# A long convolution in front of a maxout network: second and third transform stage of batches 1 to 3 as 64x64 products

## The chip, the cores and the metric

The kernel runs on one core of a Trainium2 chip. The metric is the device time of one launch in microseconds (us); less is better. The engines of the core are TensorE (PE in the profile, with its weight loads as PEld), VectorE (DVE), ScalarE (ACT), GpSimd (POOL) and SyncE (SP, which here only issues transfers).

## The reference

A causal convolution over the whole sequence of 12544 positions, for each of 128 channels and 4 batches, gated by x, and then a maxout network on each of the 50176 tokens. All arrays are float32.

```python
batch, seq, d_model, filter_order = 4, 12544, 128, 64
h_filt = (np.maximum(pos_emb @ w1, 0) @ w2) * np.exp(-0.01 * pos)[:, None]
u = x * v
Uf, Hf = rfft(u, n=2 * S, axis=1), rfft(h_filt, n=2 * S, axis=0)
y = irfft(Uf * Hf[None], n=2 * S, axis=1)[:, :S]
a = (x * y).reshape(50176, 128)
out = np.maximum(np.maximum(a @ moe_w1, a @ moe_w2), a @ moe_w3) @ moe_w_out   # 768 hidden units
```

## The kernel before

**The transform.** The sequence is seen as 98 blocks of 128 positions. The first stage (`u_first`, `first_halves`) is a product over the 98 blocks into 90 frequencies; its result lies in the tile `spec`, 128 partitions by 90 frequencies by 2 by 128 channels. The second stage runs over the 128 partitions (real and imaginary part of 64 values) for two frequencies at a time, a pair; there are NK = 45 pairs in a batch. For a pair `g_second` makes eight products of 128x64 by 128 columns (`halves_mm`: two products of 64 output rows each, one beside the other), `g_butterfly` adds and subtracts the halves, `g_swap` (two copies on ACT), `g_re` and `g_im` multiply by the filter's spectrum, `g_unfold` adds and subtracts again, and `g_third` makes eight products back. Its result goes to DRAM (`zd`, one tile for each batch). The last stage, `t_last`, takes four positions by 98 blocks of one batch from there (`t_load`: the `zt` part from `zd` and `xT`, the part of x), makes sixteen short products and multiplies by x. That tile of 392 tokens, `gt`, is what the network works on.

**The network.** A tile has six slots, one for each 128 of the 768 hidden units. In a slot `up` makes two products of 392 columns (`pa`, `pb`); ACT takes the relu of the one and DVE the maximum with the other, and `down`, one slot later, adds the third product to the output's PSUM tile `ops` (with `lin` once in a tile). There are NT = 32 tiles in a batch.

**The order.** Instructions stand in the order of the program (`manual_schedule`); each engine does its own in that order. Batch 0 is transformed by itself in a prologue, to about 320 us, together with the filter's spectrum, which goes to `hd` in DRAM. In that stage `s_filter` makes sixteen products of 64x64 by 128 columns for each pair. After that the tiles of batches 0, 1 and 2 run, and beside the tiles of batch b the transform of batch b + 1: `conv_steps` hands out a list of steps for each of the batch's 192 slots, and the main loop runs them after the slot's `up` and `down`. Its places come from one line and a few offsets: the first stage of the 32 column groups u (26 in batch 1, six are done in the prologue) one after the other, then the pairs.

```python
per_pair = 170 / (NK + 0.6 * (NU - done))
s0 = int((NU - done) * 0.6 * per_pair) + 10
s = s0 + int(g * per_pair)
at(s - 5, 0, w_load, g, 0); at(s - 3, 0, h_load, g); at(s, 1, g_second, g)
at(s + 1, 0, w_load, g, 1); at(s + 1, 0, g_butterfly, g); at(s + 2, 0, g_swap, g)
at(s + 3, 0, g_re, g); at(s + 4, 0, g_im, g, True); at(s + 6, 0, g_unfold, g)
at(s + 7, 1, g_third, b, g)
```

Loads are issued by SP (`u_load`, `w_load`, `h_load`, `t_load`, the transposes of `u_dma`), the stores of `zd` and of the output by ACT. The first-stage, second-stage, third-stage and `t_last` results share a pool of four PSUM buffers (`cps`, 512 columns each); `pa` and `pb` share three; `ops` has one. The tiles of batch 3 run last, in pairs of tiles, with a form of the network that has fewer products and sums on POOL.

In batches 1 to 3, `g_third` forms sum and difference of its two halves on its way out, so that `t_last` can use them as they come. For batch 0 `t_sums` does that after the load, on POOL.

Of the kernel before, what the change touches and what calls it, by code (L numbers as in the profile page):

```python
# [15 lines left out]
P = 128  # L16
# [24 lines left out]
def tables(NB):  # L41
# [4 lines left out]
    f1 = np.concatenate([a.real, a.imag], 1)  # L46
    f1h = np.zeros((64 + HH, 2 * N1))
    f1h[:HH], f1h[64:] = f1[:HH], f1[HH:NH]
    f4 = np.stack([a.T.real, a.T.imag], 1) / S
    f4p = f4[::2].transpose(1, 0, 2).reshape(N1, NB // 2, 2).transpose(0, 2, 1)  # L50
    j, t = np.arange(64), np.arange(64)
# [13 lines left out]
    both = both.reshape(N1 // 2, P, 2, 512)  # L65
    f32 = np.float32
    return f1.astype(f32), f1h.astype(f32), f4p.astype(f32), np.ascontiguousarray(both, f32)
# [3 lines left out]
def kernel(  # L71
# [32 lines left out]
    zd = [dram.tile([N1, 2, 64, 256], FP32, name=f"zd{b}") for b in range(B)]  # L104

    f1_t, f1h_t, f4p_t, w_t = tables(NB)
# [3 lines left out]
    wt_d = nc.inline_tensor(w_t, name="wt_const").ap()  # L110
    order = 127 - (2 * np.arange(64)[None, :] + np.arange(2)[:, None]).ravel()
# [6 lines left out]
    f1 = const.tile([NB, 2 * N1], FP32, name="f1")  # L118
# [153 lines left out]
    nc.gpsimd.dma_start(f1[:], f1_d)  # L272
# [40 lines left out]
    us, uts, ws, hts, eos, xts, xss, abs_, pss = ({} for _ in range(9))  # L313

    def pools(b, u):
        if b == 0:
            return inp0 if u % 2 else inp
        return inp if u < EARLY or u % 5 < 3 else inq
# [20 lines left out]
    def u_turn(u):  # L339
        if u % 2 == 0:  # L340
            uts[u] = uts[u + 1] = utp.tile([NB, 8, 2, 64], FP32, tag="uT", name="uT")
        ps = state["turn"].tile([P, 512], FP32, tag="cv", name="pst")
        turn(u, ps)
        nc.scalar.copy(uts[u][:, 4 * (u % 2):4 * (u % 2) + 4],
                       ps[0:NB, :].rearrange("n (s t r) -> n s r t", s=4, r=2))
# [16 lines left out]
    def u_join(u):  # L362
        if u % 2 == 0:
            uts[u] = uts[u + 1] = utp.tile([NB, 8, 2, 64], FP32, tag="uT", name="uT")
        t = us.pop(u)
        for h in range(2):
            copies[h](
                uts[u][:, 4 * (u % 2):4 * (u % 2) + 4].rearrange(
                    "n s r t -> n (s r t)").bitcast(U16).rearrange(
                    "n (s r t h) -> n h s r t", h=2, r=2, t=64)[:, h],  # L370
                t[0:NB, 4 * h:4 * h + 4].rearrange("n s (t r) -> n s r t", r=2))

    def u_first(u, h, copy=None):
        t = uts[u] if h == 0 else uts.pop(u)
        ps = cps.tile([P, 512], FP32, tag="cv", name="ps1")
        at = 4 * u + 2 * h
        first_halves(ps, [t[:, at % 8 + j] for j in range(2)], f1[:], spec[:, :, :, at:at + 2],
                     copy or copies[h])

    def w_load(g, a):  # L380

        w = state["pair"][0].tile([P, 2, 2, P], FP32, tag=f"w{a}", name="wt")
        nc.sync.dma_start(w[:].rearrange("p k r m -> p (k r m)"), wt_d[g, :, a, :])
        ws[g, a] = w

    def h_load(g):
        ht = state["pair"][1].tile([P, 2, 2, 2, D], FP32, tag="h", name="ht")
        for half in range(2):
            nc.sync.dma_start(
                ht[64 * half:64 * half + 64].rearrange("p c k q d -> p c (k q d)"),  # L390
                hd[g].rearrange("(c j) f -> j c f", c=2))
        hts[g] = ht

# [37 lines left out]
    def g_third(b, g):  # L431
# [7 lines left out]
        if b == 0:  # L439
            nc.scalar.copy(zs[:].rearrange("p k f -> p (k f)"), ps[:])  # L440
        else:
            z1 = state["cv"][0].tile([P, 256], FP32, tag="z1", name="z1", bufs=1)
            nc.scalar.copy(z1[:], ps[:, 256:512])  # L443
            for a, op in enumerate((ALU.add, ALU.subtract)):
                nc.vector.tensor_tensor(out=zs[:, a], in0=ps[:, 0:256], in1=z1[:], op=op)  # L445
        nc.scalar.dma_start(
            zd[b][2 * g:2 * g + 2].rearrange("k c t f -> (c t) k f"), zs[:])

    def conv_steps(b, done):
# [9 lines left out]
        per_pair = 170 / (NK + 0.6 * (NU - done))  # L459
        for u in range(done, NU):  # L460
            s = (u - done) * 0.6 * per_pair + 9
            at(max(0, int(s) - 10), 0, u_load, b, u)
# [4 lines left out]
            for h in range(2):  # L467
                at(int(s + 1 + 0.3 * per_pair * h), 1, u_first, u, h)
        s0 = int((NU - done) * 0.6 * per_pair) + 10
        for g in range(NK):  # L470
            s = s0 + int(g * per_pair)
            at(s - 5, 0, w_load, g, 0)
            at(s - 3, 0, h_load, g)
            at(s, 1, g_second, g)
            at(s + 1, 0, w_load, g, 1)
            at(s + 1, 0, g_butterfly, g)
            at(s + 2, 0, g_swap, g)
            at(s + 3, 0, g_re, g)
            at(s + 4, 0, g_im, g, True)
            at(s + 6, 0, g_unfold, g)  # L480
            at(s + 7, 1, g_third, b, g)
# [10 lines left out]
    def t_load(b, i):  # L492
        zt = hp.tile([N1, 2, 512], FP32, tag="zt", name="zt", bufs=2)
        for c in range(2):
            nc.sync.dma_start(
                zt[NK * c:NK * c + NK],
                zd[b].rearrange("(g a) c t f -> g a c t f", a=2)[
                    :, :, c, 2 * i:2 * i + 2, :].rearrange("g a t f -> g a (t f)"))
# [6 lines left out]
    def t_sums(i, eng=nc.gpsimd):  # L505
        if i[0]:
            return
# [485 lines left out]
```

## Time and profile before

| | |
|---|---|
| timed runs | 2401.75 us median of 3 (2400.04 to 2402.64) |
| profiled execution, span from first to last instruction | 2397.1 us (no other time is given for it) |
| mean granted TensorE clock | 0.997 |
| transfers | 408.43 MB, mean 170 GB/s |
| matmul groups: `pa`, `pb`, `ops` with `hid` (392 columns) | 643.5, 642.7, 481.2 us busy |
| second and third stage, all four batches (L130, `ps`) | 193.9 and 191.5 us busy, 2880 records each |
| first stage (L139, `ps`), 4096 records | 188.9 us busy |
| `sps` of `s_filter` (L788), 1440 records | 49.7 us busy |

The busy time of a group is the union of its records. Matmuls overlap, so a group's mean duration isn't what an additional one costs; the distance between the starts of groups is. A float32 matmul and its weight load show as two records each. In the views of transfers, "issue" is the time that SP or ACT spends on a transfer's instruction, and "landing" the time until its data is there. The busy shares leave these issues out.

### The profile page before, as it was taken

To read this page: it belongs to the slowest core of one execution; us is meant where nothing else is said; L and a number is where in the kernel's file an instruction comes from. 1 tells how busy PE (TensorE), PEld (TensorE's weight loads), DVE (VectorE), ACT (ScalarE), POOL (GpSimd) and SP (SyncE) were. 2 spreads that over 40 slices of the span, in tenths; PEclk is the share of its full clock that TensorE was granted. 3 is DMA by queue.
4 is the path that set the end of the run, shared out by engine and by line. 5 is a ranking of instruction groups with operands and counts; after the bars stand their busy time and mean duration, and the time that the engine had idled before them with its cause. 6 is when DMAs were issued, how large, how long until landed. Compare 5 with 4: busy or idle time off the path is not lost.

```text
span 2397.1 us, 67636 instructions
## 1 busy us (share of the span) xinstructions
PE 2366.6 (99%) x27853; PEld 1514.6 (63%) x27853; DVE 1318.5 (55%) x2806; ACT 1018.9 (43%) x1978; POOL 704.1 (29%) x775
## 2 busy tenths in 40 slices
PE   9999999999999999999999999999999999999998
PEld 7889856656555556666655546666665645666665
DVE  5588844466666645446666644546666643333333
ACT  2688834444444434444444424444444432222222
POOL 2055432222323211101111111101111105666666
PEclk9999999999999999999999999999999999999999
DMA  7778978868787659968778859978778842222221
GB/s 173 178 230 269 278 162 173 171 185 215 205 215 208 181 128 189 182 172 211 215 206 215 216 129 182 180 165 216 214 210 220 203 134 55 68 56 55 66 64 21
DMA packets 532221, 408.43 MB, mean 170 GB/s; under 512 B 375859, under 2 KB 421996, under 8 KB 531913
## 3 DMA queue, kind: packets, MB, share of 16 engines
q1 hardware_dynamic: 422240, 315.25, 55.0%
q10 hardware_dynamic: 100233, 67.88, 9.8%
q0 software_dynamic: 9440, 20.98, 3.6%
q8 instruction: 219, 3.59, 0.6%
q14 instruction: 89, 0.73, 0.1%
HBM read 295.69 MB, written 84.67 MB: 159 GB/s over the span
## 4 chain that ended last, share of the span: by engine, by line
PE 91%; ACT 3%; DMA 2%; issue 1%; DVE 1%; POOL 1%; ACTq 0%; SPq 0%; POOLq 0%; DVEq 0%
PE pb L130 21%; PE pa L130 21%; PE ops L130 18%; PE ps L130 11%; PE ps L139 7%; PE ops L601 5%; PE yps L130 5%; ACT ht L793 1%; PE pm L299 1%; DMA hd<-ht 1%; PE pst L337 1%; PE pw L130 1%; ACT zs L440 1%; PE gps L770 0%; ACT xs L409 0%
## 5 line engine op out<-in xcount | busy, mean ns | idle before, releaser
L541 DVE TENSOR_TENSOR hid<-hid,pb 128x392 f32<-128x392 f32 x768 | 431.4, 562 | 725.9 <-PE pb L130 492.2
L538 ACT ACTIVATE hid<-pa 128x392 f32<-128x392 f32 x768 | 381.8, 498 | 789.6 <-PE pa L130 616.3
L130 PE MATMUL pb<-gt,w_sb 128*64 128x392 f32 x3072 | 642.7, 494 | 4.4 <-ACT hid L538 4.2
L130 PE MATMUL pa<-gt,w_sb 128*64 128x392 f32 x3072 | 643.5, 494 | 0.8 <-DVE gt L528 0.8
L130 PE MATMUL ops<-hid,wo_sb 128*64 128x392 f32 x2304 | 481.2, 492 | 0.0
L420 POOL TENSOR_TENSOR xt<-xt,xs 128x512 f32<-128x512 f32 x135 | 172.5, 1278 | 889.8 <-DVE xs L419 662.8
L130 PEld LDWEIGHTS pb<-gt,w_sb 128*64 128x64 f32 x3072 | 227.7, 137 | 286.1 <-issue 251.0
L130 PEld LDWEIGHTS ops<-hid,wo_sb 128*64 128x64 f32 x2304 | 173.4, 137 | 205.8 <-issue 162.0
L130 PEld LDWEIGHTS pa<-gt,w_sb 128*64 128x64 f32 x3072 | 202.9, 137 | 61.5 <-issue 34.3
L139 PEld LDWEIGHTS ps<-f,uT 98*64 98x64 f32 x4096 | 178.5, 137 | 47.5 <-issue 44.0
L130 PEld LDWEIGHTS ps<-ab,wt 128*64 128x64 f32 x2880 | 166.2, 137 | 48.0 <-issue 30.3
L130 PEld LDWEIGHTS ps<-spec,wt 128*64 128x64 f32 x2880 | 171.9, 137 | 38.7 <-issue 34.8
L130 PE MATMUL ps<-spec,wt 128*64 128x128 f32 x2880 | 193.9, 273 | 1.9 <-issue 1.4
L130 PE MATMUL ps<-ab,wt 128*64 128x128 f32 x2880 | 191.5, 274 | 0.0
L352 POOL COPY planes<-ut 128x784 uint16<-128x784 uint16 x90 | 76.3, 848 | 388.8 <-DVE ut L332 246.1
L139 PE MATMUL ps<-f,uT 98*64 98x90 f32 x4096 | 188.9, 241 | 0.4 <-ACT zs L440 0.3
L445 DVE TENSOR_TENSOR zs<-ps,z 128x256 f32<-128x256 f32 x270 | 101.9, 419 | 96.7 <-ACT z L443 94.5
L130 PEld LDWEIGHTS yps<-f4p,zt 90*64 90x64 f32 x3584 | 134.0, 138 | 25.9 <-issue 22.0
L409 ACT ACTIVATE xs<-xt 64x512 f32<-64x512 f32 x180 | 113.1, 629 | 71.7 <-DVE xt L156 58.9
L427 DVE TENSOR_TENSOR ab<-xt 128x256 f32<-128x256 f32 x360 | 135.9, 419 | 4.5
L130 PE MATMUL yps<-f4p,zt 90*64 90x49 f32 x3584 | 137.3, 221 | 0.4 <-DVE zt L511 0.4
L528 DVE TENSOR_TENSOR gt<-yps,xT 128x392 f32<-128x392 f32 x128 | 72.5, 566 | 111.3 <-PE yps L130 62.3
(114 smaller groups left out, 2544.5 us busy)
## 6 DMA issues: line engine op xcount, KB each, us to landing
wt<-wt_const SPq DMA_DIRECT2D x360, 256.0 KB, 4.8
ht<-hd SPq DMA_DIRECT2D x270, 256.0 KB, 4.9
zd<-zs ACTq DMA_DIRECT2D x180, 256.0 KB, 4.7
zt<-zd SPq DMA_DIRECT2D x256, 180.0 KB, 4.2
ut<-in_xr_dram SPq DMA_DIRECT2D x128, 196.0 KB, 3.7
ut<-in_vr_dram SPq DMA_DIRECT2D x128, 196.0 KB, 4.1
xT<-in_x_dram SPq DMA_DIRECT2D x512, 49.0 KB, 2.8
out_dram<-ot ACTq DMA_DIRECT2D x96, 196.0 KB, 4.4
```

Source lines behind the costliest of these rows:

```text
L130: nc.tensor.matmul(out[64 * h:64 * h + 64], lhsT[:, 64 * h:64 * h + 64], rhs, start=start, stop=stop, skip_group_check=True)
L139: nc.tensor.matmul(ps[64 * c:64 * c + 64, 256 * i + r * N1:256 * i + (r + 1) * N1], a[:, r, :], table[:, c * N1:(c + 1) * N1], start=(i % ...
L299: nc.tensor.matmul(ps[64 * h:64 * h + HH, 512 * r + q * FO:512 * r + (q + 1) * FO], posv[64 * h:64 * h + 64, P - 1 - 2 * (8 * i + q) - r, ...
L352: nc.gpsimd.tensor_copy(pl_[:, :, :, 0:NB], a[:].bitcast(U16).rearrange("p s (n h) -> p h s n", h=2))
L409: nc.scalar.mul(xs[0:64], xt[64:128], -1.0)
L420: (nc.gpsimd if apart else nc.vector).tensor_tensor(out=xt[:], in0=xt[:], in1=xs[:], op=ALU.add)
L427: nc.vector.tensor_tensor(out=ab[:, :, q, :], in0=y[:, :, 0, :], in1=y[:, :, 1, :], op=op)
L445: nc.vector.tensor_tensor(out=zs[:, a], in0=ps[:, 0:256], in1=z1[:], op=op)
L528: nc.vector.tensor_tensor(out=g[:].rearrange("d p (m a) -> d p m a", a=2), in0=y, in1=xT[:].rearrange("d p (m a) -> d p m a", a=2), op=ALU ...
L538: nc.scalar.activation(h[:], pa[:, 0:N], Relu)
L541: nc.vector.tensor_tensor(out=h[:], in0=h[:], in1=pb[:, 0:N], op=ALU.max)
L601: nc.tensor.matmul(ps[64 * c:64 * c + 64, 0:H2], w, rhs[:, H2 * c:H2 * c + H2], start=start, stop=True, skip_group_check=True)
```

## The change

For batches 1 to 3 the two middle stages are written with radix 4. The first stage sums its two halves of 64 positions as they leave PSUM (`u_first`: one copy on ACT, a sum and a difference on DVE), so that the second stage is four products of 64x64 for a frequency in place of four of 128x64. For that the 128 partitions of a pair of `spec` are put into another order by four SBUF-to-SBUF transfers (`q_load`). `g_quarter` makes the second stage of pair g and the third stage of pair g - 3 in one step, in one PSUM tile of two banks; `g_fold` takes both out with one copy and two sums. `h_load` has four transfers in place of two, `q_swap` four copies of 32 partitions in place of two of 64, `w_load` 128 KB in place of 256. `zd` of these batches has another order, so `t_load` has four `zt` transfers in place of two, and `t_sums` is needed for them: on POOL for the first 16 tiles, on DVE with a sign for each partition for the other 16. The pool `cps` has two buffers of 1024 columns in place of four of 512. Batch 0 keeps its form. The diff, cut to its core:

```diff
+    j, t = np.arange(32), np.arange(32)
+    quarter = [[], []]
...
-    zd = [dram.tile([N1, 2, 64, 256], FP32, name=f"zd{b}") for b in range(B)]
+    zd = [dram.tile([N1, 2, 64, 256] if b == 0 else [N1, 2, 32, 2, 256], FP32, name=f"zd{b}")
+          for b in range(B)]
...
-    def u_first(u, h, copy=None):
...
+    def u_first(u, i0=0, n=4):
+        t = uts[u] if i0 + n < 4 else uts.pop(u)
+        ps = cps.tile([P, 256 * n], FP32, tag="cv", name="ps1")
+        at = 4 * u + i0
+        for i in range(n):
+            for h in range(2):
+                for c in range(2):
+                    nc.tensor.matmul(
+                        ps[64 * c:64 * c + 64, 256 * i + h * N1:256 * i + (h + 1) * N1],
+                        t[:, 2 * ((at + i) % 8) + h].rearrange("n r t -> n (r t)"),
+                        f1q[:, h, c * N1:(c + 1) * N1],
+                        start=(i % 2 == 0 and h == 0), stop=True, skip_group_check=True)
...
+        nc.scalar.copy(high, v[:, 0])
+        for a, op in enumerate((ALU.add, ALU.subtract)):
+            nc.vector.tensor_tensor(out=spec[:, :, a, at:at + n], in0=v[:, 1], in1=high, op=op)
 
     def w_load(g, a):
-        w = state["pair"][0].tile([P, 2, 2, P], FP32, tag=f"w{a}", name="wt")
-        nc.sync.dma_start(w[:].rearrange("p k r m -> p (k r m)"), wt_d[g, :, a, :])
+        w = wp.tile([P, 2, 2, 64], FP32, tag=f"w{a}", name="wt")
+        nc.sync.dma_start(w[:].rearrange("p k r m -> p (k r m)"), wq_d[g, :, a, :])
         ws[g, a] = w
 
+    def q_load(g):
+        t = wp.tile([P, 2, 2, D], FP32, tag="sq", name="sq")
+        for r in range(2):
+            for c in range(2):
+                nc.sync.dma_start(
+                    t[64 * r + 32 * c:64 * r + 32 * c + 32].rearrange("p k a d -> p (k a d)"),
+                    spec[64 * c + 32 * r:64 * c + 32 * r + 32, 2 * g:2 * g + 2].rearrange(
+                        "p k a d -> p (k a d)"))
+        sqs[g] = t
+
     def h_load(g):
-        ht = state["pair"][1].tile([P, 2, 2, 2, D], FP32, tag="h", name="ht")
-        for half in range(2):
-            nc.sync.dma_start(
-                ht[64 * half:64 * half + 64].rearrange("p c k q d -> p c (k q d)"),
-                hd[g].rearrange("(c j) f -> j c f", c=2))
+        ht = hh.tile([P, 2, 2, 2, D], FP32, tag="h", name="ht")
+        for a in range(2):
+            for half in range(2):
+                at = 64 * a + 32 * half
+                nc.sync.dma_start(
+                    ht[at:at + 32].rearrange("p c k q d -> p c (k q d)"),
+                    hd[g].rearrange("(c j s) f -> s j c f", c=2, s=2)[a])
         hts[g] = ht
+
+    def g_quarter(g, z):
+        ps = cps.tile([P, 1024], FP32, tag="cv", name="psq")
+        if g is not None:
+            w, t = ws.pop((g, 0)), sqs.pop(g)
+            for k in range(2):
+                for r in range(2):
+                    for a in range(2):
+                        at = 512 * r + k * D
+                        nc.tensor.matmul(
+                            ps[64 * a:64 * a + 64, at:at + D], w[64 * r:64 * r + 64, k, a, :],
+                            t[64 * r:64 * r + 64, k, a, :], start=(k == 0), stop=True,
+                            skip_group_check=True)
+        if z is not None:
+            w, ab = ws.pop((z, 1)), abs_.pop(z)
...
+    def g_fold(g, z):
+        ps = pss.pop((g, z))
+        lo, hi = 0 if g is not None else 256, 512 if z is not None else 256
+        eo = cvp.tile([P, 512], FP32, tag="eo", name="eo", bufs=2)
+        nc.scalar.copy(eo[:, lo:hi], ps[:, 512 + lo:512 + hi])
+        cb = cvp.tile([P, 2, 512], FP32, tag="cb", name="cb", bufs=3)
+        for a, op in enumerate((ALU.add, ALU.subtract)):
+            nc.vector.tensor_tensor(out=cb[:, a, lo:hi], in0=ps[:, lo:hi], in1=eo[:, lo:hi],
+                                    op=op)
...
+    def g_store(b, z):
+        nc.scalar.dma_start(
+            zd[b][2 * z:2 * z + 2].rearrange("k c t a f -> (k c t) a f"), zss.pop(z))
+
+    def q_swap(g):
+        xt = xts[g]
+        xs = cvp.tile([P, 2, 2, D], FP32, tag="xs", name="xs", bufs=3)
+        for at in (0, 64):
+            nc.scalar.mul(xs[at:at + 32], xt[at + 32:at + 64], -1.0)
+            nc.scalar.copy(xs[at + 32:at + 64], xt[at:at + 32])
+        xss[g] = xs
...
+    LATE = 3
...
-        per_pair = 170 / (NK + 0.6 * (NU - done))
+        per_pair = 170 / (NK + LATE + 0.6 * (NU - done))
...
+            at(int(s + 1), 1, u_first, u)
+        s0 = int((NU - done - 1) * 0.6 * per_pair + 9) + 5
+        for x in range(NK + LATE):
+            s = s0 + int(x * per_pair)
+            g, z = x if x < NK else None, x - LATE if x >= LATE else None
+            at(s, 1, g_quarter, g, z)
+            at(s + 1, 0, g_fold, g, z)
+            if z is not None:
+                at(s - 4, 0, w_load, z, 1)
+                at(s + 2, 0, g_store, b, z)
+            if g is None:
+                continue
+            at(s - 3, 0, q_load, g)
+            at(s - 4, 0, w_load, g, 0)
+            at(s - 2, 0, h_load, g)
+            at(s + 2, 0, q_swap, g)
+            at(s + 3, 0, q_re, g)
+            at(s + 4, 0, q_im, g)
+            at(s + 6, 0, q_unfold, g)
...
     def t_load(b, i):
...
+            q, j = divmod(i, NT // 2)
+            for a in range(2):
+                nc.sync.dma_start(
+                    zt[NK * c:NK * c + NK, a].rearrange("g (t f) -> g t f", t=2),
+                    zd[b].rearrange("(g a) c t q f -> g a c t q f", a=2)[
+                        :, a, c ^ (a & q), 2 * j:2 * j + 2, q, :])
...
     def t_sums(i, eng=nc.gpsimd):
-        if i[0]:
-            return
         z0, z1 = zts[i]
-        even = hp.tile([N1, 512], FP32, tag="even", name="even", bufs=1)
-        eng.tensor_tensor(out=even[:], in0=z0, in1=z1, op=ALU.add)
-        eng.tensor_tensor(out=z1, in0=z0, in1=z1, op=ALU.subtract)
+        even = hp.tile([N1, 512], FP32, tag="even", name="even", bufs=2)
+        if i[0] == 0 or i[1] < NT // 2:
+            eng.tensor_tensor(out=even[:], in0=z0, in1=z1, op=ALU.add)
+            eng.tensor_tensor(out=z1, in0=z0, in1=z1, op=ALU.subtract)
+        else:
+            for out, op in ((even[:], ALU.add), (z1, ALU.subtract)):
+                nc.vector.scalar_tensor_tensor(out=out, in0=z1, scalar=sign_t[:, 0:1], in1=z0,
+                                               op0=ALU.mult, op1=op)
...
-    cps = conv.enter_context(tc.tile_pool(name="cps", bufs=4, space=PSUM))
+    cps = conv.enter_context(tc.tile_pool(name="cps", bufs=2, space=PSUM))
...
-            if f == 1:
-                t_sums(tiles[n + 1])
+            turn_ = i == NT - 1
+            if f == (3 if turn_ else 1):
+                t_sums(tiles[n + 1], nc.vector if turn_ else nc.gpsimd)
```

## The prediction

> **What bounds the kernel now.** I read the page first. TensorE (PE) is busy in every slice and the granted clock is full, so what counts is which PE instructions there are and whether anything makes PE wait.
>
> ```profile
> PE 2366.6 (99%) x27853; PEld 1514.6 (63%) x27853; DVE 1318.5 (55%) x2806; ACT 1018.9 (43%) x1978; POOL 704.1 (29%) x775
> ...
> PE   9999999999999999999999999999999999999998
> ...
> PE 91%; ACT 3%; DMA 2%; issue 1%; DVE 1%; POOL 1%; ACTq 0%; SPq 0%; POOLq 0%; DVEq 0%
> ```
>
> The third line is the chain that ended last: 91% PE. The other engines have slack, 64% for VectorE (DVE) and 44% for ScalarE (ACT) in the window 1060 to 1400 us, where batch 2 is transformed beside the tiles of batch 1. PE's timeline in such a window gives the prices, start to start; a matmul shows as two records.
>
> ```profile
> 1202.59 1.04 PE L130 MATMUL ps<-spec,wt 128*64 128x128 f32 x16
> 1203.47 0.83 PE L130 MATMUL pa<-gt,w_sb 128*64 128x392 f32 x4
> ...
> 1205.44 0.83 PE L130 MATMUL pa<-gt,w_sb 128*64 128x392 f32 x4
> ...
> 1207.42 1.09 PE L130 MATMUL yps<-f4p,zt 90*64 90x49 f32 x32
> 1208.34 1.06 PE L130 MATMUL ps<-ab,wt 128*64 128x128 f32 x16
> 1209.22 0.83 PE L130 MATMUL pa<-gt,w_sb 128*64 128x392 f32 x4
> ```
>
> A slot (`up` and `down` of one f) is 1.97 us, the eight matmuls of `g_second` or `g_third` 0.88, `t_last` 0.92; `lin` adds 0.66 (one product, a third of a slot). A tile of six slots is 11.82 + 0.92 + 0.66 = 13.40 us and the pairs in it: `conv_steps` places one per 170/(45 + 19.2) = 2.65 slots, 2.27 a tile at 2 x 0.88. Sum 17.39; the trace's `lin` products at 1201.28, 1219.09 and 1236.02 are 17.37 apart on average. So the sum works.
>
> **What is removed from PE.** Sixteen products of 128x64 per pair become sixteen of 64x64, with as many columns. Batch 0's `s_filter` already does sixteen 64x64 products of 128 columns:
>
> ```profile
> 196.03 1.06 PE L130 MATMUL ps<-spec,wt 128*64 128x128 f32 x15
> 197.02 1.10 PE L788 MATMUL sps<-w2x,G 64*64 64x128 f32 x32
> 198.05 1.09 PE L130 MATMUL ps<-ab,wt 128*64 128x128 f32 x16
> 198.97 0.27 PE L770 MATMUL gps<-wt,specH 128*64 128x128 f32 x1
> ```
>
> Its 32 records start within 0.83 us (the last record lasts about 0.27 of the 1.10), so four products run at once, twice the density of the others. But the group before it takes 1.10 from its first full record (the first of its 16 began at 195.92) where 0.88 is usual, and it takes 1.03 itself: 0.22 is lost going into the 64x64 form and 0.17 coming out. I price a full `g_quarter` at 1.03 + 0.22 = 1.25 us and one with a single half at 1.25 - 0.44 = 0.81. Per batch the steps were 90 x 0.88 = 79.2 us; they become 42 x 1.25 + 6 x 0.81 = 57.4. That is 21.8 us a batch and 65 us for three. Nothing else of PE changes: `u_first` keeps its sixteen 90-column matmuls.
>
> [...]
>
> **What is added to the SP queue.** SP issues the loads one after another, and this is where the change is dear. In the build, a pair of batches 1 to 3 has `w_load` 2 (before 2), `h_load` 4 of 32 partitions (before 2 of 64) and the new `q_load` 4 of 32; a tile of batches 1 to 3 has `zt` 4 (before 2) and `xT` 4.
>
> ```profile
> L389 SPq DMA_DIRECT2D ht<-hd x270: 573/607/1648, 464.1 to 1927.8; - x135
> ...
> L383 SPq DMA_DIRECT2D wt<-wt_const x270: 325/430/2117, 463.4 to 1933.0; - x135
> ...
> L495 SPq DMA_DIRECT2D zt<-zd x256: 812/860/1598, 314.4 to 2328.2; - x128
> ...
> L502 SPq DMA_DIRECT2D xT<-in_x_dram x512: 311/430/1657, 316.4 to 2330.6; - x171
> ```
>
> These are the views by source line: issue time in ns, least, median, most. About 0.05 us lies between two issues. Before, a pair costs 2 x 0.61 + 2 x 0.43 + 0.2 = 2.3 and a tile 2 x 0.86 + 4 x 0.43 + 0.3 = 3.7, so 2.27 x 2.3 + 3.7 = 8.9 of 17.39 us: half. After, the new pieces of 32 partitions have no row of their own; `xT` has 32 partitions too, so I take 0.43 (ends: 0.31, its least, and 0.61, the `ht` row). A pair is 10 x 0.43 + 0.5 = 4.8, a tile 4 x 0.86 + 4 x 0.43 + 0.4 = 5.56. The pairs now come every 170/(48 + 19.2) = 2.53 slots, 2.37 a tile: SP needs 2.37 x 4.8 + 5.56 = 16.95 us. PE needs 13.40 + 2.37 x 1.25 = 16.36. So SP is late by 0.59 a tile over 45 x 2.53/6 = 19 tiles, 11 us a batch, for batches 2 and 3: 22 us. Batch 1 is transformed beside the tiles of batch 0, whose `zt` stays at two transfers (3.74 a tile) and whose pairs come every 2.67 slots: 2.25 x 4.8 + 3.74 = 14.5 of 16.2, which PE hides. At the low end SP fits everywhere (13.7 a tile): 0. At 0.61 it needs 20.3: 150 us for two batches and 31 for batch 1.
>
> [...]
>
> **The rest, off PE.** ACT: `q_swap` has four copies of 512 elements instead of two. Copies of 512 take 0.591 us on 98 partitions (L344) and 0.592 on 128 (L440), so 32 partitions save nothing: +1.25 us a pair; the two evictions of 256 (0.373 each) become one of 512 (0.59). Per pair of 2.53 slots ACT has 1.26 of relu, 0.59, 2.48 of swaps, 0.38 for issuing the store and 0.37 for its share of output copies: 5.1 us of 6.90, 74%. Behind the swaps on ACT stands the next relu, needed only when `down` runs after the next `up`, about 1.5 us later: priced at 0. Without that cover, 0.5 us in each of 135 pairs, 67. DVE: `g_fold`, two of 512 at about 0.70 (L415), replaces four of 0.42; `u_first` gains about 0.6 us each; `t_sums` adds 2 x 0.69 (L510) in half of the tiles: in summed durations from 5.64 of 7.68 us a pair to 5.58 of 6.90, so the busy share goes from 64% to about 71%; 0. POOL: two sums of 1.29 us in the other half, with two slots before `t_last` as in batch 0, where PE lost 2.2 us in all; 2 us. Four PSUM buffers of one bank become two of two: a buffer is free after the copy and two sums (1.9 us), and the third user comes a slot and a `t_last` (2.9 us) later at the closest; 0, or 0.5 x 270 = 135 if evictions are held up. The last phase has DVE at 36%: its 60 added `t_sums` cost 0.
>
> **Sum.** 2397.1 - 65 + 22 + 2 = 2356 us of span. The profile gives its execution by its span alone; the timed runs' median is 4.65 above it, so 2361.
>
> **Rivals.** *PE-bound throughout* (SP issues at its least times, or works ahead into its buffers of three): 2397.1 - 65 + 4.65 = 2337. For it: in the transform's first part SP's issues already fill 0.75 to 0.78 of the time (summed over 50 us pieces of its timeline) and PE's row stays at 9.
>
> *Transfers in order through eight semaphores, slower.* The build rotates all SP and ACT transfers over DMAHW0 to 7, so a transfer waits for the landing of the eighth before it, and ACT's `g_store` stands in that order with relu behind it. SP shows the wait already, on ACT's stores:
>
> ```profile
> SPq L495 <- DMA zd<-zs: 161.7, 26, 25.1
> ...
> SPq L502 <- DMA out_dram<-ot: 83.3, 30, 3.9
> ```
>
> In the window 1060 to 1400 the median times to landing are 3.7 us (`xT`, 49 KB), 5.3 (`ht`, 256 KB), 4.8 (store), 4.4 (out). Between them I estimate 3.8 for 64 KB, 4.0 for `zt`, 4.3 for 128 KB. A pair then holds semaphores for 2 x 4.3 + 4 x 3.8 + 4 x 4.3 + 4.8 + 0.42 x (4 x 4.0 + 4 x 3.7 + 4.4) = 60.6 us; over eight, 7.6 us, 18.0 a tile where PE needs 16.36: +62 for two batches, and +8 for batch 1 by the same sum. Then 2337 + 70 + 2 = 2409, and each microsecond a tile that ACT waits for SP's late transfers in the 58 tiles adds 58: 2409 to 2450. It decides once the mean time to landing passes 4.1 us. Against it: smaller transfers spread evenly should land sooner; at the whole run's medians (2.8 to 4.9) the need is 6.4 us and fits.
>
> [...]
>
> **Chances.** SP-bound 0.32, PE-bound 0.20, the semaphores 0.42, density 0.03, other 0.03. A measurement of this kernel can tell about 0.2%, 5 us. The first two give nearly all of faster, 0.50; same 0.08; slower 0.42. The forecast's own range is 2345 to 2390 (half the SP term to twice it, and some relu waits); with both rivals 2335 to 2445, which leaves out the density case and the 0.61 price.
>
> **What would show it.** `psq` groups of 32 records at 0.027 us with about 0.4 around them; tiles of 16.2 us beside batch 0 and 16.9 beside batches 1 and 2; SP's issues back to back there, PE's waits ending at `sq` or `wt`. Right for PE-bound: 16.4 throughout. Right for the semaphores: 18 or more, ACT idle before stores, PE waiting for `hid`. I am wrong if PE waits for PSUM or relu while SP is idle.

## The result and the profile after

The changed kernel takes 2807.9 us (median of 4 runs, 2798.4 to 2812.1), the kernel before 2401.3 in the same series: a ratio of 1.169 (95% interval 1.167 to 1.171). The forecast was 2361 us, with a range of 2335 to 2445. It was wrong in its direction and in its range. The mean granted clock fell from 0.997 to 0.934.

The page of the changed kernel, the rows that answer to those of before, with the clock's row:

```profile
PE 2482.6 (88%) x27853; PEld 1448.5 (52%) x27853; DVE 1488.0 (53%) x2798; ACT 1171.2 (42%) x2124; POOL 783.3 (28%) x835
...
PE   9999899888888899978777799998777778999998
...
PEclk9999999988898999988888999998898889999999
```

PE, at 9 in every slice before, has three dents: the stretches in which the pairs of batches 1, 2 and 3 are worked on. PE is idle for 2805.9 - 2482.6 = 323 us, where it was 30.5. And its busy time rose by 116 us, though it has less to do: the clock row has 8s in the same slices. No other engine is near its limit. The waits of PE and of SP (what waited, for what, us in total, times, longest) tell what PE stands for:

```profile
PE psq L454 <- DMA sq<-spec: 253.3, 120, 4.9
PE ops L151 <- DVE hid L673: 22.1, 36, 2.0
PE pb L151 <- ACT hid L670: 14.8, 38, 3.2
```

```profile
SPq L428 <- DMA zd<-cb: 129.3, 55, 3.7
...
SPq L419 <- DMA out_dram<-ot: 76.1, 17, 5.3
...
SPq L419 <- DMA zd<-cb: 69.2, 18, 5.5
```

PE waits for `sq`, the re-laid spectrum. SP, which should load it, isn't short of time (its issues fill 0.60 to 0.68 of the pair stages): it stands at `q_load` (L428) and `w_load` (L419) until a *store* has landed, one of `zd` or of the output, with which the load has nothing to do but the semaphore. The timeline of one pair, all engines (start, duration, engine, line, operation, count, idle time before):

```profile
643.16 0.67 PE L454 MATMUL psq<-sq,wt 64*64 64x128 f32 x16
...
647.80 0.58 ACT L476 COPY eo<-psq 128x512 f32<-128x512 f32 x1
...
649.68 1.28 DVE L479 TENSOR_TENSOR cb<-psq,eo 128x512 f32<-128x512 f32 x2
...
651.00 0.52 ACTq L487 DMA_DIRECT2D zd<-cb  x1
...
651.46 3.52 SPq L428 DMA_DIRECT2D sq<-spec  x4
...
654.44 0.69 PE L454 MATMUL psq<-sq,wt 64*64 64x128 f32 x4 [1.15 <-DMA sq<-spec]
...
656.51 0.91 PE L454 MATMUL psq<-sq,wt 64*64 64x128 f32 x10 [1.38 <-DMA sq<-spec]
...
658.41 1.57 PE L151 MATMUL pa<-gt,w_sb 128*64 128x392 f32 x4
```

Read it as a ring. The joint step runs at 643.16. ACT takes its result out at 647.80, since it has its own stores and the swap of the pair before ahead of it; DVE folds at 649.68; ACT issues the store at 651.00, and it lands at 653.81. SP has issued two of the next pair's four `sq` at 651.46 and 652.08; the third has the store's semaphore and starts at 653.83, 0.02 us after the landing. It and the fourth land at 655.74 and 656.38, and PE goes on at 656.51: 13.4 us from one joint step to the next. In the build, of the loads of `sq` and `wt` that come eighth after a transfer of ACT, 55 stand behind the `zd` store of the pair just before, 18 behind the one before that, and 29 behind an output store. ACT's stores hardly ever wait there themselves: in the trace all but one of them start 1.9 us or more after the landing that they would have to wait for.

The last line above is a second effect: `pa` took 1.36 us until the next group, where 0.66 is usual. The clock record has 0.5 from 654.46 to 661.29. There are 65 such records of 3.4 to 10.2 us, 372 us in all, and 60 of them begin in the pair stages.

The step itself, where nothing makes it wait, and the issue times of SP (least, median, most in ns), which answer to the rows of before:

```profile
1313.07 0.82 PE L151 MATMUL ops<-hid,wo_sb 128*64 128x392 f32 x4
...
1313.82 0.67 PE L454 MATMUL psq<-sq,wt 64*64 64x128 f32 x16
1314.31 0.62 PE L464 MATMUL psq<-xs,wt 64*64 64x128 f32 x16
1314.86 0.88 PE L151 MATMUL pa<-gt,w_sb 128*64 128x392 f32 x4
```

```profile
L428 SPq DMA_DIRECT2D sq<-spec x540: 507/588/1837, 479.8 to 2325.7; - x180
...
L439 SPq DMA_DIRECT2D ht<-hd x540: 302/427/1699, 482.6 to 2327.9; - x180
...
L624 SPq DMA_DIRECT2D zt<-zd x384: 315/411/1841, 970.9 to 2737.3; - x192
```

The step takes 1314.86 - 1313.82 = 1.04 us between the starts and some 0.1 more ahead of it (0.75 from the start of the `ops` group to the step, where such a group takes 0.66 elsewhere): 1.13 us, less than the 1.25 of the forecast. So PE has what the change promised; it doesn't get its operands.

A table that will be used below: for each run the distances from the start of a group to the start of the next one on PE, summed by group, less the same sum of the kernel before. A wait shows in the group ahead of it.

| | `psq`, second and third stage | `pa` | `pb` | `ops` with `hid` | `yps` | all |
|---|---|---|---|---|---|---|
| changed | +95 | +64 | +61 | +110 | +75 | +409 |
| e1 | -57 | +15 | +40 | +35 | +18 | +57 |
| e8 | -92 | +17 | +35 | +15 | +7 | -14 |
| e10 | -93 | +67 | +54 | +17 | +4 | +53 |
| e12 | -92 | +8 | +15 | +14 | +5 | -46 |

### The profile page after: what moved, and what is told of

It reads as the page before. It is cut to its first block, busy times and chain, and to the rows that moved or that the text cites. A ratio compares the mean times of both kernels' runs of the same rounds, so it can differ in the third digit from the quotient of the medians.

```text
span 2805.9 us, 69204 instructions
## 1 busy us (share of the span) xinstructions
PE 2482.6 (88%) x27853; PEld 1448.5 (52%) x27853; DVE 1488.0 (53%) x2798; ACT 1171.2 (42%) x2124; POOL 783.3 (28%) x835
## 5 line engine op out<-in xcount | busy, mean ns | idle before, releaser
L151 PE MATMUL pb<-gt,w_sb 128*64 128x392 f32 x3072 | 673.9, 517 | 15.8 <-ACT hid L670 14.8
L151 PE MATMUL ops<-hid,wo_sb 128*64 128x392 f32 x2304 | 500.4, 512 | 22.5 <-DVE hid L673 22.1
L507 POOL TENSOR_TENSOR cb<-cb,xs 128x512 f32<-128x512 f32 x135 | 174.3, 1291 | 1232.1 <-DVE xs L504 799.9
L454 PE MATMUL psq<-sq,wt 64*64 64x128 f32 x2160 | 146.6, 326 | 258.5 <-DMA sq<-spec 253.3
L494 ACT ACTIVATE xs<-cb 32x512 f32<-32x512 f32 x270 | 169.4, 627 | 241.3 <-DVE hid L673 193.1
L415 DVE TENSOR_TENSOR spec<-ps,high 128x360 f32<-128x360 f32 (+1 forms) x204 | 142.3, 740 | 91.9 <-ACT high L413 91.4
L479 DVE TENSOR_TENSOR cb<-psq,eo 128x512 f32<-128x512 f32 (+1 forms) x288 | 174.8, 648 | 12.7 <-ACT eo L476 12.6
L495 ACT COPY xs<-cb 32x512 f32<-32x512 f32 x270 | 166.2, 615 | 3.2
L404 PEld LDWEIGHTS ps<-f1q,uT 98*64 98x64 f32 x3072 | 133.7, 137 | 34.3 <-issue 29.0
L404 PE MATMUL ps<-f1q,uT 98*64 98x90 f32 x3072 | 138.1, 241 | 3.0 <-DVE spec L415 2.6
L464 PE MATMUL psq<-xs,wt 64*64 64x128 f32 x2160 | 129.2, 323 | 0.0
L151 PE MATMUL yps<-f4p,even 90*64 90x49 f32 x2048 | 125.8, 220 | 2.5 <-DMA f4p<-f4p_const 2.5
```

What stands on the lines that cost most here:

```text
L151: nc.tensor.matmul(out[64 * h:64 * h + 64], lhsT[:, 64 * h:64 * h + 64], rhs, start=start, stop=stop, skip_group_check=True)
L404: nc.tensor.matmul(ps[64 * c:64 * c + 64, 256 * i + h * N1:256 * i + (h + 1) * N1], t[:, 2 * ((at + i) % 8) + h].rearrange("n r t -> n (r ...
L415: nc.vector.tensor_tensor(out=spec[:, :, a, at:at + n], in0=v[:, 1], in1=high, op=op)
L454: nc.tensor.matmul(ps[64 * a:64 * a + 64, at:at + D], w[64 * r:64 * r + 64, k, a, :], t[64 * r:64 * r + 64, k, a, :], start=(k == 0), stop ...
L464: nc.tensor.matmul(ps[64 * k:64 * k + 64, at:at + D], w[64 * a:64 * a + 64, k, q, :], ab[64 * a:64 * a + 64, q, k, :], start=(g is None an ...
L479: nc.vector.tensor_tensor(out=cb[:, a, lo:hi], in0=ps[:, lo:hi], in1=eo[:, lo:hi], op=op)
```

## Experiments: what holds the loads up

The kernel before took 2399 to 2402 us (medians) in all these series. Theory A is the ring through the store. Its rivals: B, SP's issue time; C, the loads stand too late in the list; D, PE or PSUM. e2 to e6 and e10 are single runs, the others medians of four to ten; the four runs of the changed kernel lie within 14 us.

**e1, both stores issued by POOL.**

```diff
 def g_store(b, z):
-        nc.scalar.dma_start(
+        nc.gpsimd.dma_start(
 def down(i, f, h):
-        nc.scalar.dma_start(dst, o[:])
+        nc.gpsimd.dma_start(dst, o[:])
```

> g_store and the output's store are issued by POOL instead of ACT; POOL's transfers have semaphores of their own, so no ACT transfer stands in the rotation of eight any more. All of SP's loads, their number and order of issue stay. Theory A (a load of pair x has to wait for the landing of the store of pair x-1, eight places before it in the rotation, so that every pair runs as one serial chain): the chain is cut, 2330 to 2400 us, tiles beside batches 1 and 2 at 16.4 to 17.5 us in place of 25.5. Theory B (SP's issue time is the bound): nothing it depends on changes, 2780 to 2830.

Measured: 2459.2 us (2454.6 to 2461.6), ratio 1.024 (1.023 to 1.026); clock 0.990. Two words on the issuing engine take away 349 of 407 us, and SP has as much to issue as before. B alone is out. But A had expected 2330 to 2400 and doesn't explain all; e8 takes up the rest. PE's wait for `sq` is 47.8 us instead of 253.3:

```profile
PE psq L454 <- DMA sq<-spec: 47.8, 50, 2.4
```

**e2, the loads two or three slots earlier in the list** (`q_load` and `w_load` at s - 6, `h_load` at s - 4). What it changes in the computation: the first pairs re-lay the spectrum before its last columns are in.

> The loads are asked for two or three slots sooner (q_load and both w_load at s - 6, h_load at s - 4); stores stay on ACT. In the built program 52 pieces of sq and wt still have the store of the pair before in their semaphore. Theory A: the chain is the same, 2740 to 2840 us. A theory C, that the loads simply stand too late in the list for their landing: 2350 to 2500.

Measured: 2835.6 us where the changed kernel takes 2807.9, no gain. To load earlier in the list was of no use here, where the queue stands at a semaphore: C alone is out.

**e3, no re-laying**: the products read `spec` in place.

```diff
 def q_load(g):
-        t = wp.tile([P, 2, 2, D], FP32, tag="sq", name="sq")
...
-        sqs[g] = t
+        sqs[g] = spec[:, 2 * g:2 * g + 2]
```

> q_load moves nothing; g_quarter reads spec where it lies, so the re-laying of the spectrum is left out (540 transfers less, everything else as in the changed kernel). Theory A: the rotation comes round slower in the list (19 pieces of wt still wait for a store, two pairs back), 2340 to 2430 us. Theory B: SP has 330 us less to issue, about the same fall. A theory D, that PE's 64x64 steps themselves or the PSUM pool are what costs: stays above 2600.

Measured: 2453.7 us, clock 0.994. The stores are on ACT as in the change; with four transfers fewer a pair the rotation falls differently (19 places behind a `zd` store of two pairs before, 2 behind an output store), and there is little to wait for that has to come late. The joint steps and the PSUM pool are those of the change, so D (above 2600) is out. A and B aren't parted here, since SP has 540 issues less; A's range (2340 to 2430) was missed by 24 us.

**e4, only the store of `zd` on POOL.**

> Only g_store goes to POOL; the output's store stays on ACT and in the rotation (12 pieces of sq and wt wait for one). Theory A: the chain through the pairs is cut, 2335 to 2430 us, a little above the kernel with both stores on POOL. Theory B: 2780 to 2830.

Measured: 2640.3 us, outside of what A had expected (2335 to 2430). The output's store still stands ahead of loads in the rotation, in 12 places of `sq` in the build, and ahead of loads of `zt` (L624) and `xT` (L631), behind which SP issues the next `sq`:

```profile
PE psq L454 <- DMA sq<-spec: 150.1, 99, 4.1
```

```profile
SPq L624 <- DMA out_dram<-ot: 92.4, 22, 7.8
...
SPq L428 <- DMA out_dram<-ot: 69.3, 12, 6.6
...
SPq L631 <- DMA out_dram<-ot: 53.0, 26, 3.6
```

Both stores take part: the output's store, all that e4 differs by from e1, is worth 181 us.

**e10, only the loads of `ht` on POOL; both stores stay on ACT.** It moves no store. It changes who stands eight places behind whom, and takes four issues a pair from SP.

```diff
 def h_load(g):
-                nc.sync.dma_start(
+                nc.gpsimd.dma_start(
```

> The changed kernel with the four loads of ht of each pair issued by POOL; both stores stay on ACT. This moves the places in the rotation of the eight semaphores: of the loads of sq and wt whose eighth predecessor is an ACT transfer, 55 stood behind the zd store of the pair just before and now none does: 53 stand behind the store of three pairs before, 16 of four pairs before, 56 behind an output store. Theory A (what makes the time is the loop through the store of the pair just before, and not that ACT issues stores): 2420 to 2600 us, the output stores' places being what is left. Rival (any ACT store in the rotation holds SP up as long): above 2640 us, as in e4, where 12 output stores were left in such places.

Measured: 2454.2 us, clock 0.997. In the profile of e10 the wait is gone (group of PE, busy and mean, idle time before it and its releaser):

```profile
L454 PE MATMUL psq<-sq,wt 64*64 64x128 f32 x2160 | 91.4, 282 | 1.1 <-DMA sq<-spec 1.1
```

The change has 258.5 us there. This is the clearest run for A: the same stores, issued by the same engine at the same places of the program, and 354 us less, since a load now comes after a store that is three pairs old. It takes 1.7 us of issues a pair from SP as well, so A's share was not parted from B's in this run alone; e1, where SP kept all its loads, does that. Output stores still hold SP up in e10, for 125 us at `sq` and `xT` (83.4 and 41.2), and PE loses nothing by it. So these waits of SP cost nothing here, where SP has four issues a pair less, while in e4 they did: behind a store that is not part of the ring, SP's wait reaches PE only when SP has no time to spare, as far as these two runs tell.

What stays lies elsewhere, in `pa` and `pb`, and has the sign that the prediction gave to the semaphores:

```profile
PE pb L151 <- ACT hid L670: 47.7, 91, 3.2
```

In e8 below, where POOL issues the stores, that wait is 7.5 us and the kernel 61 us faster. ACT spends 135 x 0.54 = 72 us on issuing the `zd` stores, ahead of the ReLU; that this is the cause was not tested by itself.

**e6, work for PE ahead of the step.** Is the slow clock a cause of its own, or only a mark of the waiting?

```diff
 def g_quarter(g, z):
         ps = cps.tile([P, 1024], FP32, tag="cv", name="psq")
+        flat = wo_sb[:].rearrange("p c d -> p (c d)")
+        for n_ in range(4):
+            halves_mm(ps[:, 512 * (n_ % 2):512 * (n_ % 2) + N], w_sb[1][:, 0:P], flat[:, 0:N],
+                      True, True)
```

> The changed kernel with four more 392 column products, of no use to the output, at the start of every joint step of second and third stage: 4 pairs of products of 0.66 us each, 2.6 us a step and some 380 us over the 144 steps at full clock. They stand on PE just ahead of the place where it waits for sq. Theory C2 (the idle time before that wait is what halves the clock, and the slow products after it cost about 200 us): PE doesn't idle there, the granted clock goes from 0.934 to over 0.97, pa groups of 1.3 us fall back to 0.66, and in spite of 380 us more work the time is 2680 to 2850 us. Rival (the clock has another cause, or costs nothing on the path): the clock stays below 0.95 and the time is 2900 to 3150 us.

Measured: 2779.4 us, clock 0.993. In the page and the groups of e6:

```profile
PE 2704.7 (97%) x30157; PEld 1549.9 (56%) x30157; DVE 1493.2 (54%) x2798; ACT 1174.5 (42%) x2124; POOL 781.4 (28%) x835
...
PEclk9999999999999999999999999999999999999999
```

```profile
L151 PE MATMUL psq<-wo_sb,w_sb 128*64 128x392 f32 x2304 | 404.0, 493 | 0.0
```

404 us of products that nobody needs, and the kernel is 28 us *faster*. They fill the time in which PE would wait, the clock stays full, and `pa` and `pb` fall from +64 and +61 us over the kernel before to +8 and +16. So the waiting costs PE twice: some 290 us of idle time, and 150 to 200 us for working at half the clock. The upper end is 116 + 82 = 198 (its busy time rose by 116 where the shorter steps should have taken 82 away); against e6 without its useless products it is 2482.6 - (2704.7 - 404.0) = 182; and PE is busy for 298 of the 372 us at half the clock, half of which is 149.

## Experiments: what is left without the ring

**e5, e1 and e3 together** (no re-laying, stores on POOL; no load stands behind a store of ACT).

> The changed kernel with both relations between the loads and the stores taken away: the spectrum isn't re-laid (the products read its rows in place, so the output has the second stage's rows exchanged), and the store of zd and the output's store are issued by POOL. In e3 without the re-laying 2453.7 us were measured, 52 us above the kernel before, with about 21 loads whose eighth predecessor in the rotation was still an ACT store. Theory A whole (what is left above the kernel before is those last waits for landings): 2350 to 2400 us. Rival E (what is left are waits in the order of ACT and DVE themselves, the swap behind the fold and the ReLU behind the swap, priced at 0 in the prediction with 67 us as bound): 2435 to 2460 us, PE's idle time before pb and ops as in e3 (34 and 31 us).

Measured: 2393.9 us, in the range of "theory A whole" at its upper end. Rival E in the form given there is out. But 2350 was not reached; e8, which is as fast and leaves nothing of the computation out, shows why.

**e8, e1 with the loads of `ht` on POOL too** (the edit of e10).

> e1 (both stores issued by POOL, 2459.2 us) with the four loads of ht of each pair issued by POOL as well: SP has 4 x 0.43 = 1.7 us less to issue per pair, 230 us over 135 pairs. Theory B (in e1 what is left is SP's issue time: 48 us of PE's waiting for sq and the clock that falls behind it): 2380 to 2420 us, PE's wait for sq under 10 us. Rival E (what is left are ACT's and DVE's waits in their own order): 2440 to 2465 us. Rival F (POOL, which has the sums of the zt planes and the adds, becomes late with 8 issues a pair): above 2470 us.

Measured: 2393.2 us (2389.7 to 2396.1), ratio 0.9974 (0.9963 to 0.9985): by 0.3% the first version that beats the kernel before. B's range for what was left in e1 was met, and PE's wait for `sq` is down to 1.8 us: SP's issues were worth 66 us in e1 (the `ht` loads leave the rotation too, which this run doesn't part from them). Its `psq` steps take 92 us less than before, but `pa`, `pb` and `ops` take 67 more, some 14 of it the 0.1 us ahead of 144 steps. The waits of ACT and DVE in e8 name what lies there:

```profile
ACT xs L494 <- DVE cb L479: 201.0, 121, 2.8
```

```profile
DVE hid L673 <- ACT hid L670: 272.5, 126, 2.7
```

ACT comes to the swap, waits for DVE's fold, makes four copies of 0.62 us, and only then the next ReLU, for which DVE's max and then PE's `ops` wait.

**e12, the swap in two copies of 64 partitions instead of four of 32.** It leaves the right order of the swapped rows out.

```diff
 def q_swap(g):
-        for at in (0, 64):
-            nc.scalar.mul(xs[at:at + 32], xt[at + 32:at + 64], -1.0)
-            nc.scalar.copy(xs[at + 32:at + 64], xt[at:at + 32])
+        nc.scalar.mul(xs[0:64], xt[64:128], -1.0)
+        nc.scalar.copy(xs[64:128], xt[0:64])
```

> e8 with the swap in two copies of 64 partitions instead of four of 32 (so the swapped rows are exchanged between the halves of each half, and the output with them): ACT has 2 x 0.63 us less in each of 135 pairs, and the ReLU behind the swap comes 1.26 us earlier. In e8 PE's steps of second and third stage take 92 us less than before, but its groups of pa, pb and ops together 66 us more, pb's 35 of it, and it ends behind ReLU and max. Theory E1 (those 66 us come from ACT, the ReLU behind four swaps): 2340 to 2370 us. Rival E2 (they come from DVE's own order, the max behind the fold and the multiplies): 2380 to 2395 us.

Measured: 2358.8 us (2356.7 to 2361.4), ratio 0.983 (0.981 to 0.984), in E1's range. By the table `pa` and `pb` come down from +17 and +35 to +8 and +15. In the profile of e12 DVE's wait for the ReLU is 111.6 us instead of 272.5:

```profile
DVE hid L672 <- ACT hid L669: 111.6, 92, 2.3
```

**e15 and e17, one or two of the four copies on DVE** (`nc.vector` instead of `nc.scalar`); **e16, one of them on POOL.**

> e8 with the fourth of the swap's four copies on DVE instead of ACT: ACT has 0.62 us less per pair, DVE some 0.4 more, in order behind the fold. e12 took two copies away and gained 34 us, 17 each. Theory E1 (ACT's work ahead of the ReLU counts, DVE's is hidden): 2370 to 2385 us. Rival E2 (DVE's order counts as much): 2388 to 2410 us.

> e8 with the third and the fourth of the swap's four copies on DVE instead of ACT (e15 moved the fourth alone and gained 16.5 us, 2393.2 to 2376.7). DVE's busy share in the pair stages was already 0.8 to 0.9 in e15. Theory E1 (ACT's work ahead of the ReLU counts, DVE's stays hidden, as in e12, which reached 2358.8 us with two copies left out): 2357 to 2368 us. Rival E2 (DVE is now as full as ACT was, and the max and the fold come late): 2375 to 2410 us.

> e8 with the fourth of the swap's four copies on POOL instead of ACT: ACT has 0.62 us less per pair, POOL some 0.6 to 1.3 more, behind its issues of stores and of ht. Theory E1: 2370 to 2385 us. Rival F (POOL issues in order and waits for ACT's output copy, 263 us in e8, so its copy comes late and the multiply on DVE waits for it): 2395 to 2440 us.

Measured: e15 2376.7 us (ratio 0.990, 0.989 to 0.992), e17 2374.8 (0.989, 0.988 to 0.991), e16 2396.7 (0.998, 0.997 to 0.999). The first copy that ACT is rid of gains 16.5 us, as E1 said. The second gains 2, where E2 (2375 to 2410) has its lower end: by then DVE is the later one. Its wait for ACT's ReLU, 111.3 us in e15, is gone in e17:

```profile
DVE hid L674 <- ACT hid L671: 10.2, 19, 0.6
```

POOL takes the copy (0.64 us each) but not in time, as rival F had it: DVE then waits 50.9 us for it. e17 and e15 are the fastest versions here that leave nothing of the computation out.

**e13, DVE rid of `t_sums` beside the pairs** (plain adds without the sign; those of 32 tiles of batches 1 and 2 go to POOL, those of batch 3 stay on DVE).

> e8 with the sums of the zt planes of all tiles as plain adds on POOL (without the sign of half of the planes, so the second half of the tiles of batches 1 to 3 has them exchanged in places): DVE has 48 x 2 x 0.90 = 87 us less to do beside the pairs of batches 2 and 3, POOL that much more. Theory E2 (the max waits in DVE's own order): 2355 to 2385 us, with DVE's part of the waits before ops falling. Rival E1: 2385 to 2395 us. Rival F (POOL, which issues stores and loads of ht here, becomes late): above 2400 us.

Measured: 2400.6 us, 7 more than e8, in the range of rival F (POOL late). What DVE has to do as a whole isn't what counts: `pa`, `pb` and `ops` still take 62 us more than before (e8 67), and the `yps` groups, which wait for these sums, took 11 us more than in e8.

**e9 and e14, the swap a slot later.** Both aimed at ACT's wait for the fold; e14 has a fourth buffer for `xs` and one less for `eo`.

> e8 with the swap one step later (s+3), the multiply by the imaginary part and the unfolding one step later too (s+5, s+7), and so the third stage four pairs back instead of three: three more joint steps and as many more slots in the run. In e1 ACT waits 195 us for DVE's fold at the swap (135 times, 1.45 us each), with a ReLU behind it each time. Rival E (these waits are what is left): 2340 to 2400 us, ACT's wait for the fold under 60 us. If they are hidden behind PE's work: within 10 us of e8, or up to 15 us above it for the longer tail of each batch.

> e9 (e8 with swap, multiply and unfolding a slot later and the third stage four pairs back) with a fourth buffer of xs and, to make room for it, one of eo and high instead of two. In e9 (2456.9 us) ACT's wait before the swap moved from the fold to PE's psq, 160 us: with four pairs in the pipe and three buffers of xs the swap had to wait until the third stage had read its buffer. Theory E3 (what is left in e8 is the place of the swap, its wait for the fold): that wait goes without a new one, 2345 to 2380 us. Rival E1 (it is the work that ACT has per pair, wherever it stands): 2385 to 2410 us.

Measured: 2456.9 and 2421.6 us, both slower than e8 and outside of every range expected. Each time the wait only moved. In e9 ACT waits for the buffer of `xs`, in e14 DVE's multiply, which overwrites what the swap reads, waits for the swap:

```profile
ACT xs L494 <- PE psq L464: 159.7, 63, 6.5
```

```profile
DVE cb L499 <- ACT xs L495: 143.5, 101, 3.1
```

So they don't tell whether a later place alone would help. That stays open; that the amount of work ahead of the ReLU counts is shown by e12 and e15.

## Why the prediction was wrong

- **The ring, the step that failed.** The sum priced SP's loads by their issue time alone (+22 us) and had nothing for a load that has to wait for a store of ACT. That wait makes most of the 407 us: e1, which takes the stores out of the order and leaves SP all its loads, is 349 us faster. The rival "transfers in order through eight semaphores" named the right mechanism: a load waits for the landing of the eighth transfer before it (in the trace the third `sq` starts 0.02 us after the store's landing at 653.81), and ACT's store stands in that order. Its size was wrong, by its model. It took the semaphores as a *throughput* (time held, over eight: +70 us) and had it decide "once the mean time to landing passes 4.1 us" (by its own figures that comes earlier: PE's 6.90 us a pair times eight, over 14.8 transfers, is 3.7). The transfers land in 2.0 (`sq`) to 2.7 us (`ht`, `wt`, the store), far inside that, and it decided all the same. What counted isn't how long a semaphore is held but *what comes before the transfer that holds it*: the store is issued only after the step, ACT's copy and DVE's fold of the pair before, so the rotation closes a ring step, copy, fold, store, landing, load, landing, step. The tiles beside batch 0 take 23.6 us instead of 16.2, those beside batches 1 and 2 25.2 instead of 16.9. e1 and e10 break the ring in two different ways and take 349 and 354 us away. The profile of before had the sign of it, SP waiting for stores of ACT, 161.7 and 83.3 us, though some 80 of the 161.7 are the first loads of a batch, which wait for the `zd` that they read. The order of the build, which tells which store stands eight places ahead of which load, was not followed up pair by pair.
- **The clock.** No step of the prediction had it. Half the clock in the 65 stretches cost 150 to 200 us (e6). In the trace of the changed kernel no long gap comes before the fall at 654.46: the longest was 1.15 us. What the falls have in common there is the sum: in the 3.4 us before each of the 65 (the length of the shortest of them), PE was idle for at least 1.57 us in all (1.59 at 654.46).
- **PE's step: right, and mis-sized.** Four products do run at once between the 392-column products (the sixteen of a step in 1.04 us between the starts, where eight took 0.88 before), so the density case of the chances, the new products at the rate of the old, is out. 1.13 us instead of 1.25 makes the gain 82 us instead of 65 (0.1 us goes into the 64x64 form and not 0.22).
- **SP's term: mis-sized.** An `sq` piece takes 0.59 us to issue, not 0.43, a `zt` piece 0.41, not 0.86; the sum of a tile, 2.37 x (4 x 0.59 + 4 x 0.43 + 2 x 0.38 + 0.5) + 4 x 0.41 + 4 x 0.43 + 0.4 = 16.4 us, is close to the 16.95 forecast, by luck, since two errors cancel. But SP also waits, so e8 found 66 us where the forecast had 22. For `sq` the issue is 0.59 us of the 2.0 to the landing.
- **ACT behind the swap: priced at 0, bound 67.** The copies cost 0.62 us as forecast, but the ReLU isn't covered: about 52 us in e8, 34 of which go with two of the copies (e12). The bound held, the cover wasn't there.
- **DVE, POOL, PSUM at about 0: right**, as far as e8 shows it (`yps` +7 us; PE waits for no PSUM buffer). The 64% and 44% that the prediction calls slack are the busy shares of DVE and ACT. A `t_sums` instruction on DVE takes 0.90 us on average, not 0.69. The last phase kept its steps of 11.2 and 14.8 us.
- **The signs named in advance.** Tiles of "18 or more" came. "PE waiting for `hid`" came only in small (22.1 and 14.8 us): PE waited for `sq`, which the text had given to the SP-bound case.

Without the ring and with SP relieved, the prediction's terms with their measured sizes, 2397.1 - 82 (steps) + 52 (ReLU and max) + 7 (`yps`) = 2374, come within 13 us of e8's span of 2386.9. By the table and the spans these 13 lie in three places of 4 to 5 us each: the steps (92 less the 14 ahead of them is 78 and not 82), groups that the table doesn't list, and the time behind PE's last product.

## What to carry to other kernels

Before a transfer is added to a queue, write out the rotation of its semaphores as it stands in the built program (here eight, for all transfers of SP and ACT), with the transfers of *all* engines that share it, and look for a load that follows a store: if that store needs the result of a step that needs such a load, it is a ring, and its time is a sum of latencies (here 13.4 us for the pair shown), though the queue isn't full (here SP's issues filled 0.60 to 0.68 of the time). Break it by issuing the stores (or some of the loads) elsewhere, not by loading earlier. And look at the clock before pricing a wait of PE: here 290 us of idle time brought 150 to 200 us more at half the clock.

## What the runs showed of the hardware

- In the trace of the changed kernel the clock's 65 records of 0.5 are 3.4 us (23 of them), 6.8 (39), 10.2 (two) or 6.6 (one) long. With its stretches at full clock cut into pieces of 3.4 us too, each of the 65 falls follows a piece in which PE was idle for 1.57 to 3.41 us, in however many gaps. Of the 647 pieces that no fall follows, six have 1.60 to 2.00 us, so the two overlap and this trace shows no limit.
- Filling such gaps with useless products made a kernel faster (e6: 404 us more work, 28 us less time; the mean granted clock 0.993 where the changed kernel had 0.934).
- Issuing a piece of 32 partitions on SP took 0.59 us SBUF to SBUF (`sq`) and 0.43 from DRAM (`ht`), medians of the changed kernel; on POOL an `ht` piece took 0.54 to 0.60 (means: e10 542 ns, e16 545, e15 587, e12 603).
- Copies of 512 elements took as long on 32 partitions (0.62 us on ACT in the changed kernel, 0.64 on POOL in e16) as on 64 (0.62 on ACT before).
